# A Fourier mixing layer and a gated feed-forward layer on one core: when the filters and the last third of the weights are loaded, and how many filler matmuls run

## The chip, the cores and the metric

The kernel runs on one core of one Trainium2 chip. The metric is the device time in microseconds (us) of one execution. The time before is 983.68 us, the median of 4 runs (981.99 to 984.23).

The engines are named as in the profile: PE is the matrix engine (TensorE), DVE the vector engine, ACT the scalar engine, POOL the GpSimd engine, and SP the engine that issues most of the DMA transfers.

## The reference, cut to what matters

```python
# x: (8, 3008, 256); filt_r, filt_i: (1505, 256)
X = np.fft.rfft(x, axis=1)
Y = X * (filt_r + 1j * filt_i)[None]
y = np.fft.irfft(Y, n=3008, axis=1).reshape(24064, 256)
out = np.maximum(y @ w_gate, 0.0) * (y @ w_val) @ w_out    # w_gate, w_val: (256, 1536), w_out: (1536, 256)
```

## The kernel before

The transform of length 3008 is done as 94 x 32, in matmuls. For each of the 8 batches, stage A multiplies x by a table of cosines and sines (`psA`) and stores the result to DRAM (`Abuf`). It is loaded again in another order, in four slabs (`at`). This round trip is called the bounce of A. Stage B makes the second transform (`psX`), multiplies by the filters (`tt`, `uu`) and transforms back (`psD`). A second bounce through DRAM (`Dbuf`, `dC`) leads to stage C (`psY`). Then come the matmuls of the feed-forward layer (`psV`, `psG`, `psO`).

From batch 1 on, all this is woven into the feed-forward matmuls of the batch before. Batch 0 has nothing to hide behind. The change concerns only this start, which I call the prologue.

The parts that matter:

```python
    def load_filters(half):            # 8 DMAs per half (half 0 has 4 small ones more), fp32 -> bf16, issued by POOL
        ...
                nc.gpsimd.dma_start(dst[r:r + 31:2, gs, :], ...)
                nc.gpsimd.dma_start(dst[r + 1:r + 32:2, gs, :], ...)
        ...
    def place_filters(half):           # the other rows are a copy of these
        ...
                if half == 0:
                    nc.vector.tensor_copy(dst[r + 32:r + 64, gs, :], dst[r:r + 32, gs, :])
                else:
                    nc.sync.dma_start(dst[r + 32:r + 64, gs, :], dst[r:r + 32, gs, :])
        ...
    def load_vg(c):                    # one third of w_val and of w_gate, issued by POOL
        ...
    def hold_gpsimd(tile_):            # a tiny copy: POOL, and all that it issues later, waits for this tile
        scr = pro.tile([32, 8], tile_.dtype, tag="scr", bufs=1)
        nc.gpsimd.tensor_copy(scr, tile_)
        ...
    def items_b(b, junk=0):            # stage B, 12 items
        ...
            nc.vector.tensor_tensor(tt, psX, Ftr[:, g:g + 2, :], op=ALU.mult)
            if b == 0 and g % 4 == 2:  # every second item: uu on POOL, by way of ACT
                xs = pro.tile([128, 2, D], FP32, tag="xs", bufs=2)
                nc.scalar.copy(xs, psX)
                nc.gpsimd.tensor_tensor(uu, xs, Fti[:, g:g + 2, :], op=ALU.mult)
            else:
                nc.vector.tensor_tensor(uu, psX, Fti[:, g:g + 2, :], op=ALU.mult)
        ...
    def warm(n):                       # n matmuls on constants, to keep PE's clock up
        ...
    load_x(0, nc.sync, 2 * q)
    ...
    hold_gpsimd(XF[0][0:32, 0:8])      # the first slice of x
    load_filters(0)
    load_filters(1)
    ...
    hold_gpsimd(ats[0][64:96, NG - 1, 0:8])      # the third slab of the bounce of A
    load_vg(0)
    load_vg(1)
    for f in items_b(0, 2):
        f()
    warm(26)
    load_d(0)
    hold_gpsimd(dCs[0, 0][0:32, 0, 0:8])         # the first slice of the bounce of D
    load_vg(2)
    load_o()
    load_x(1, nc.gpsimd)
```

## Time and profile before

| what | before |
|---|---|
| time, median of 4 runs | 983.68 us |
| span of the profiled run | 980.1 us |
| stage A, PE back to back | 7.9 to 24.9 us |
| bounce of A, PE idle for 8.55 us of it | 25.5 to 37.9 us |
| stage B | 38.0 to 54.4 us |
| bounce of D | 55.3 to 59.8 us |
| wait for the last third of the weights ends | 68.2 us |
| from 80 us on | PE without gaps |

First the page of the kernel before: the busy times of the engines, the clock that was granted to PE in 40 slices of the span (9 is 90% or more), and the shares of the chain of work that ended last.

```profile
PE 962.2 (98%) x6817; PEld 664.2 (68%) x6820; DVE 577.2 (59%) x1046; ACT 556.6 (57%) x1191; POOL 51.8 (5%) x86
...
PEclk9899999999999999999999999999999999999999
...
PE 96%; DMA 2%; issue 1%; DVE 0%; ACT 0%; POOL 0%; SPq 0%; POOLq 0%; ACTq 0%
```

PE is busy for 98% of the span, and the chain is PE for 96%. Only the first slices can give anything.

Next the chain of waits of the kernel before in the first 90 us, in order of time: start, duration, and what the chain passed through.

```profile
25.52 6.19 DMA Abuf_71<-asb
...
33.55 4.28 DMA Fti<-Fti
...
37.96 0.58 PE psX L274 x2
...
54.07 5.72 issue
...
60.69 7.45 DMA WgT<-in_moe_w_gate_dram
...
68.18 0.49 PE psG L345 x2
```

The chain leaves PE at three places. Two DMAs follow each other in the bounce of A. (The one called `Fti<-Fti` is named by its place in the queue; the matmul `psX` after it needs the last slab `at`, which landed at the same time.) "issue" at 54.07 is the bounce of D, during which PE runs filler. And the load of `WgT` ends at 68.14 us.

Now PE's timeline of the same run: start, duration, engine, line, operation; in brackets the idle time before and what ended it.

```profile
16.34 1.02 PE L243 MATMUL psA<-XF_89,WA 128*96 128x512 f32 x2
...
37.96 0.58 PE L274 MATMUL psX<-at,F_91 128*128 128x256 bf16 x2 [8.55 <-DMA Fti<-Fti]
...
47.00 0.27 PE L293 MATMUL psD<-tt,I2t 128*128 128x256 bf16 x1
47.24 0.27 PE L294 MATMUL psD<-uu,I2u 128*128 128x256 bf16 x1
...
68.18 0.49 PE L345 MATMUL psG<-yT,WgT 128*128 128x376 bf16 x2 [0.78 <-DMA WgT<-in_moe_w_gate_dram]
```

The second half of x (`XF_89`) is used at 16.34 us with no wait. It is loaded by three DMAs, issued at 5.91, 7.43 and 8.47 us. The view of this tile gives, of the time from issue to landing, the least, the median and the most:

```profile
L154 SPq DMA_DIRECT2D XF_89<-in_x_dram x3: 469/469/527, 5.9 to 8.5; - x3
...
DMA to landing us min/median/max: 6.0/6.8/7.7
```

Within stage B, the matmul at 47.24 starts 0.05 us after a `uu` of POOL has ended (46.03 + 1.16 = 47.19). The last line is the wait for the last third of the weights.

POOL's timeline shows when it issues what:

```profile
7.57 0.18 POOL L227 COPY scr<-XF_88 32x8 f32<-32x8 f32 x1 [3.24 <-DMA XF_88<-in_x_dram]
8.16 0.71 POOL L186 DMA_DIRECT2D Ftr<-in_filt_r_dram  x1 [0.41 <-issue]
...
18.38 0.52 POOL L192 DMA_DIRECT2D Ftr<-in_filt_r_dram  x1 [5.69 <-DVE I2t L176]
...
28.50 0.69 POOL L188 DMA_DIRECT2D Fti<-in_filt_i_dram  x1
...
46.03 1.16 POOL L281 TENSOR_TENSOR uu<-xs,Fti 128x512 bf16<-128x512 f32 x1 [1.14 <-ACT xs L280]
48.32 1.16 POOL L281 TENSOR_TENSOR uu<-xs,Fti 128x512 bf16<-128x512 f32 x1 [1.14 <-ACT xs L280]
...
59.81 0.18 POOL L227 COPY scr<-dC 32x8 bf16<-32x8 bf16 x1 [5.74 <-DMA dC<-Dbuf_79]
...
60.69 0.71 POOL L215 DMA_DIRECT2D WgT<-in_moe_w_gate_dram  x1
```

In stage B POOL makes one `uu` every 2.30 us. At 59.81 us the hold on the bounce of D is released, and only then the last third of the weights is issued.

### The profile page before, as it was taken

How to read it: one execution, taken by the hardware profiler on the slowest of the kernel's cores; microseconds unless marked ns; L12 is line 12 of the kernel's file. 1: busy time of each engine (PE TensorE's matmuls, PEld its weight loads, DVE VectorE, ACT ScalarE, POOL GpSimd, SP SyncE). 2: the span in 40 equal slices, each digit the busy share in tenths (PEclk: the TensorE clock that was granted, in tenths of full speed). 3: DMA queues.
4: the chain of work that ended last, by engine and by line, in shares of the span. 5: the costliest groups of instructions: out<-in, count | busy, mean ns of one | idle time of the engine just before them, and what ended most of it. 6: DMA issues, size and time to landing. Idle time of an engine off the chain costs nothing.

```text
span 980.1 us, 18332 instructions
## 1 busy us (share of the span) xinstructions
PE 962.2 (98%) x6817; PEld 664.2 (68%) x6820; DVE 577.2 (59%) x1046; ACT 556.6 (57%) x1191; POOL 51.8 (5%) x86
## 2 busy tenths in 40 slices
PE   8689999999999999999999999999999999999998
PEld 3355677667775677757776577765777567777776
DVE  4543486448753496536855378543875448655554
ACT  3245665556655556555655556555665555655554
POOL 5430000010000000000000100001000000000000
PEclk9899999999999999999999999999999999999999
DMA  9984924182413814156231653317332241411111
GB/s 261 202 210 145 246 59 121 49 238 67 123 50 96 211 54 129 32 144 162 76 113 32 169 132 86 103 44 223 85 103 70 60 118 54 129 33 33 33 33 48
DMA packets 96825, 107.20 MB, mean 109 GB/s; under 512 B 6212, under 2 KB 85508, under 8 KB 95108
## 3 DMA queue, kind: packets, MB, share of 16 engines
q1 hardware_dynamic: 87760, 78.97, 29.0%
q0 software_dynamic: 8576, 25.86, 10.4%
q8 instruction: 53, 0.87, 0.4%
q10 hardware_dynamic: 400, 1.20, 0.3%
q14 instruction: 36, 0.29, 0.1%
HBM read 59.31 MB, written 49.81 MB: 111 GB/s over the span
## 4 chain that ended last, share of the span: by engine, by line
PE 96%; DMA 2%; issue 1%; DVE 0%; ACT 0%; POOL 0%; SPq 0%; POOLq 0%; ACTq 0%
PE psO L365 26%; PE psV L345 25%; PE psG L345 25%; PE psA L243 11%; PE psX L274 2%; PE psY L328 2%; PE psD L294 2%; PE psD L293 2%; PE psJ L382 1%; DMA WgT<-in_moe_w_gate_dram 1%; DMA Abuf_71<-asb 1%; DMA Fti<-Fti 0%; SPq L208 0%; POOL uu L281 0%; DVE XF_88 L386 0%
## 5 line engine op out<-in xcount | busy, mean ns | idle before, releaser
L350 DVE SCALAR_TENSOR_TENSOR prod<-psG,vsb 128x376 bf16<-128x376 f32 x768 | 421.4, 550 | 358.8 <-ACT vsb L348 348.3
L348 ACT CAST vsb<-psV 128x376 bf16<-128x376 f32 x768 | 363.5, 473 | 211.3 <-PE psV L345 210.0
L365 PE MATMUL psO<-WoT,prod 128*128 128x256 bf16 (+1 forms) x2304 | 375.1, 273 | 0.0
L345 PE MATMUL psV<-yT,WvT 128*128 128x376 bf16 x1536 | 370.4, 322 | 1.0 <-ACT yT L334 0.4
L345 PE MATMUL psG<-yT,WgT 128*128 128x376 bf16 x1536 | 369.8, 322 | 0.8 <-DMA WgT<-in_moe_w_gate_dram 0.8
L365 PEld LDWEIGHTS <-prod 128*128 128x128 bf16 (+1 forms) x2304 | 246.1, 110 | 89.9
L345 PEld LDWEIGHTS <-WgT 128*128 128x128 bf16 x1536 | 149.6, 97 | 96.6 <-DMA WgT<-in_moe_w_gate_dram 1.2
L345 PEld LDWEIGHTS <-WvT 128*128 128x128 bf16 x1536 | 143.2, 98 | 67.4 <-issue 54.9
L246 ACT CAST asb<-psA 96x512 bf16<-96x512 f32 x128 | 74.3, 582 | 100.7 <-PE psA L243 98.5
L296 ACT CAST dsb<-psD 128x512 bf16<-128x512 f32 x96 | 56.2, 586 | 50.4 <-PE psD L294 48.6
L370 ACT COPY osb<-psO 128x512 f32<-128x512 f32 (+1 forms) x128 | 61.6, 481 | 19.9 <-PE psO L365 13.5
L277 DVE TENSOR_TENSOR tt<-psX,Ftr 128x512 bf16<-128x512 f32 x96 | 65.4, 682 | 10.0 <-PE psX L274 10.0
L243 PE MATMUL psA<-XF_88,WA 128*96 128x512 f32 x128 | 65.4, 592 | 0.0
L243 PE MATMUL psA<-XF_89,WA 128*96 128x512 f32 x128 | 65.4, 592 | 0.0
L283 DVE TENSOR_TENSOR uu<-psX,Fti 128x512 bf16<-128x512 f32 x90 | 61.3, 681 | 0.0
L294 PE MATMUL psD<-uu,I2u 128*128 128x256 bf16 x192 | 47.1, 272 | 1.3 <-POOL uu L281 1.3
L293 PE MATMUL psD<-tt,I2t 128*128 128x256 bf16 x192 | 47.3, 272 | 0.1
L328 PEld LDWEIGHTS <-dC 96*128 96x128 bf16 x512 | 35.8, 97 | 14.8 <-issue 12.0
L274 PE MATMUL psX<-at,F_91 128*128 128x256 bf16 x192 | 37.3, 277 | 8.6 <-DMA Fti<-Fti 8.6
L328 PE MATMUL psY<-M_90,dC 96*128 96x94 bf16 x512 | 42.3, 204 | 0.0
L336 DVE CAST yT<-psY 128x376 bf16<-128x376 f32 x64 | 34.6, 541 | 12.1 <-PE psY L328 12.1
L334 ACT CAST yT<-psY 128x376 bf16<-128x376 f32 x64 | 30.2, 472 | 19.6 <-PE psY L328 19.6
(48 smaller groups left out, 205.1 us busy)
## 6 DMA issues: line engine op xcount, KB each, us to landing
out_dram<-osb SPq DMA_DIRECT2D x64, 256.0 KB, 2.2
XF_88<-in_x_dram POOLq DMA_DIRECT2D x20, 512.0 KB, 7.0
XF_89<-in_x_dram POOLq DMA_DIRECT2D x20, 512.0 KB, 6.7
out_dram<-osb SPq DMA_DIRECT2D x64, 120.0 KB, 1.9
XF_88<-in_x_dram SPq DMA_DIRECT2D x6, 256.0 KB, 4.3
XF_89<-in_x_dram SPq DMA_DIRECT2D x3, 512.0 KB, 6.8
Abuf_71<-asb SPq DMA_DIRECT2D x4, 384.0 KB, 6.1
at<-Abuf_71 SPq DMA_DIRECT2D x4, 384.0 KB, 6.4
```

The lines of the kernel that those rows point to most:

```text
L243: nc.tensor.matmul(psA[0:NROW], WA[:, :NROW], XF[c * NC2 // NX2][:, o:o + 512], start=True, stop=True)
L246: nc.scalar.copy(dst, psA[0:NROW])
L277: nc.vector.tensor_tensor(tt, psX, Ftr[:, g:g + 2, :], op=ALU.mult)
L283: nc.vector.tensor_tensor(uu, psX, Fti[:, g:g + 2, :], op=ALU.mult)
L293: nc.tensor.matmul(psD[:, i], I2t[:, g + i, :], tt[:, i], start=True, stop=False)
L294: nc.tensor.matmul(psD[:, i], I2u[:, g + i, :], uu[:, i], start=False, stop=True)
L328: nc.tensor.matmul(psY[:, j * N1:(j + 1) * N1], dCs[b, z][:, j, h * 128:(h + 1) * 128], M1, start=True, stop=True)
L345: nc.tensor.matmul(pt[:, :W], w[:, h, ft * 128:(ft + 1) * 128], yt[:, h, :], start=(h == 0), stop=(h == 1))
L348: nc.scalar.copy(vsb, psV[:, :W])
L350: nc.vector.scalar_tensor_tensor(prod, in0=psG[:, :W], scalar=0.0, in1=vsb, op0=ALU.max, op1=ALU.mult)
L365: nc.tensor.matmul(psO[:tw, t % 2], prods[ft][:, t * 128:t * 128 + tw], WoT[:, ft, :], start=(ft == 0), stop=(ft == NFT - 1))
L370: nc.scalar.copy(osb[:tw, :n], psO[:tw, :n])
```

## The change

The intent is to use the time before x has landed for the filters, to keep weights off the DMA engines while the last slab travels, to have the last third of the weights there before it is needed, and to spend fewer matmuls on keeping the clock up (four fewer in all).

```diff
--- before.py
+++ after.py
@@ -396,7 +396,6 @@
     for (src, dst) in FILT:
         for g in (H - 1, NG - 1):
             nc.vector.memset(dst[64:128, g, :], 0.0)
-    hold_gpsimd(XF[0][0:32, 0:8])
     load_filters(0)
     load_filters(1)
 
@@ -409,21 +408,22 @@
         if i % 4 == 3 and i > 3:
             load_at(0, i // 4 - 1)
     load_at(0, 3)
-    warm(20)
+    warm(26)
     place_tables(0)
     place_filters(0)
     place_tables(1)
     place_filters(1)
-    hold_gpsimd(ats[0][64:96, NG - 1, 0:8])
+    hold_gpsimd(ats[0][96:128, NG - 1, 0:8])
     load_vg(0)
     load_vg(1)
 
-    for f in items_b(0, 2):
+    for i, f in enumerate(items_b(0, 1)):
         f()
-    warm(26)
+        if i == 4:
+            load_vg(2)
+    warm(28)
     load_d(0)
     hold_gpsimd(dCs[0, 0][0:32, 0, 0:8])
-    load_vg(2)
     load_o()
     load_x(1, nc.gpsimd)
     for h in range(2):
```

## The prediction

> **What bounds it.** From 80 us on the kernel is TensorE-bound: the busy line gives PE 962.2 of 980.1 us, and the chain of waits PE 96%. The change touches only the first 72 us. There (chain of waits, timeline):
> - Stage A, 7.9 to 24.9 us: PE back to back. The last slice of x lands about 14.5 and is needed at 16.3.
> - Bounce, 25.5 to 37.9: last store of A 6.19 us, last slab load 6.2 us. PE idles 8.55 us; its clock is 0.5 from 34.3 to 41.1.
> - Stage B, 38.0 to 54.4: 2.30 us per two items, a latency loop DVE tt, ACT xs, POOL uu (1.16 us), PE psD, psX: PE waits 0.13 us for each POOL uu. Junk is not in it.
> - Bounce of D: loads land 59.8; 26 junk matmuls end at 60.05, 0.25 us later.
> - First block: PE stalls 1.3 us to 68.2 for the last third of the weights.
>
> **What the change does.**
> 1. Filters: without the hold (released 7.57) the first issue moves from 8.2 to 4.4 us, its packets from 11.4 to about 7.6. DMA is not idle there: share 0.83 to 0.97 under x, 1.2 to 1.3 later. The Trainium skill, "DMA: Bandwidth & Descriptors", "Queues, rings and completion order", says that engines round-robin between queues by packet; the trace agrees: beside x and the tables filters got 35 to 90 512-byte packets per us, nearly alone 350. So about 270 packets, 0.8 us of full-rate work, move forward; x slips up to 1 us inside its 1.8 us of slack. Filters end 1 to 1.5 us sooner, the last slab about 1.0 sooner (estimate; -0.5 to 2.5).
> 2. First weights held for the last slab: their packets began only at 38.0, so 0. POOL issues 1.9 us later, having had 1.9 us idle before its first uu: 0.
> 3. Last third of the weights inside stage B: 1.43 us of issue in a POOL gap of 1.14; 0.3 to 0.5 us on one uu, mostly absorbed. The first block's stall goes: gain 1.2.
> 4. One junk matmul per item instead of two: at the slow clock PE once held DVE up 0.59 us: gain 0.5. Period stays 2.30.
> 5. 28 junk matmuls instead of 26 before C, 0.213 us each: cost 0.4. Six more before stage B fall in idle time; PE still idles 6 us, so the clock still drops ("TensorE: Matmul & The Clock Gate", "What's actually happening": half clock after an idle window of about 3.4 us; here it fell 4.9 us after the last matmul). That costs little, as PE isn't stage B's bound.
>
> Sum: 1.0 + 1.2 + 0.5 - 0.4 = about 2.4 us, all critical.
>
> **Prediction: 981.2 us, 978.4 to 983.7 in 8 of 10. Faster by over 2%: 0.01; within 2%: 0.98; slower: 0.01.**
>
> **What would show it.** Filter issues from 4.4 us; stage A ends at 24.9 (0 to 0.5 later); first psX near 37; uu period 2.30; last psD 16 us after first psX; no weight wait in the first block; junk ends 0.6 us after D's first load; the rest 2.4 us earlier.
>
> **What would make it wrong.** x slipping past its slack and stalling stage A; filters finishing far sooner (first psX near 35, and with PE idle under 4 us no clock drop: 3 to 4 us won); weight issues delaying the uu loop; the weights' traffic slowing the stores of D.

## More of the kernel before

The filters' first DMA is issued at 8.16 us, after the hold was released; the ninth waits until 18.38, and the last goes out at 28.50.

Last, what the DMA queues moved from 4 to 15 us: packets, MB, and the time of their packets as a share of the 16 engines. q1 is the queue of SP (x and the bounce), q0 that of POOL (here the filters), q10 that of ACT (tables).

```profile
q1 hardware_dynamic: 411, 3.00, 77.2%
q10 hardware_dynamic: 81, 0.37, 9.1%
q0 software_dynamic: 200, 0.10, 6.6%
```

x has these 11 us nearly to itself; the filters have moved 200 packets of 512 bytes.

## The result, and the profile after

| | before | changed kernel |
|---|---|---|
| median (range) | 983.68 us (981.99 to 984.23, 4 runs) | 980.49 us (980.18 to 981.28, 4 runs) |
| ratio of the means | | 0.9972 (0.9954 to 0.9989) |

A ratio here is the mean time of one kernel's fast runs over that of the other's of the same rounds, so it is not quite the ratio of the medians. The change is a gain of some 2.8 us (0.28%). The total was close to the forecast of 2.4 us. The way there was not.

The chain of waits of the changed kernel in the first 90 us:

```profile
4.00 5.64 DMA XF_88<-in_x_dram
...
9.65 8.50 DMA XF_89<-in_x_dram
...
18.29 1.07 PE psA L243 x2
...
27.52 5.42 DMA Abuf_71<-asb
...
34.79 3.86 DMA Fti<-Fti
...
38.81 0.59 PE psX L274 x2
...
55.38 5.78 PE psJ L382 x26
61.16 0.18 PE psY L328 x4
```

The chain now begins with x. Its second half occupies the chain from 9.65 to 18.15 us. Stage A therefore ends 2 us later: the last store to `Abuf` begins at 27.52 instead of 25.52 us. That store and the slab load behind it are shorter than before. Yet the first `psX` comes at 38.81 us, 0.85 us later than before, not 1 us sooner as predicted. Near 61 us the chain runs through the 28 filler matmuls, which end after the data has come. The load of `WgT` is gone.

PE's timeline of the changed kernel:

```profile
18.29 1.07 PE L243 MATMUL psA<-XF_89,WA 128*96 128x512 f32 x2 [1.37 <-DMA XF_89<-in_x_dram]
...
38.81 0.59 PE L274 MATMUL psX<-at,F_91 128*128 128x256 bf16 x2 [6.10 <-DMA Fti<-Fti]
...
48.06 0.27 PE L294 MATMUL psD<-uu,I2u 128*128 128x256 bf16 x1 [0.71 <-POOL uu L281]
```

PE waits for `XF_89`. (The 1.37 us in brackets are what the profile counts as idle before the line; the start itself moved from 16.34 to 18.29 us.) The last line shows PE waiting 0.71 us for a `uu`. PE has less filler, so it reaches the wait sooner.

POOL's timeline of the changed kernel:

```profile
4.27 0.71 POOL L186 DMA_DIRECT2D Ftr<-in_filt_r_dram  x1
...
11.77 0.52 POOL L192 DMA_DIRECT2D Ftr<-in_filt_r_dram  x1 [2.97 <-DMA Ftr<-in_filt_r_dram]
...
19.36 0.51 POOL L192 DMA_DIRECT2D Fti<-in_filt_i_dram  x1 [5.97 <-DMA Ftr<-in_filt_r_dram]
...
28.54 0.60 POOL L188 DMA_DIRECT2D Fti<-in_filt_i_dram  x1
...
45.34 0.77 POOL L215 DMA_DIRECT2D WvT<-in_moe_w_val_dram  x1
46.09 0.72 POOL L215 DMA_DIRECT2D WgT<-in_moe_w_gate_dram  x1
46.83 1.18 POOL L281 TENSOR_TENSOR uu<-xs,Fti 128x512 bf16<-128x512 f32 x1
```

The first filter DMA is issued 3.9 us earlier than before. But the compiled program gives POOL's DMAs eight completion counters in turn, so the ninth issue waits for the first to land, the tenth for the second, and so on. The eleventh waits until 19.36 us, and the last goes out at 28.54 us against 28.50 before. The head start of the issues is lost by then. The last third of the weights is issued at 45.34 and 46.09 us, inside stage B, and the `uu` behind it starts directly afterwards.

The DMA queues of the changed kernel from 4 to 15 us:

```profile
q1 hardware_dynamic: 373, 2.65, 75.0%
q0 software_dynamic: 670, 0.32, 22.2%
q10 hardware_dynamic: 43, 0.20, 4.5%
```

The filters have moved 670 packets by 15 us instead of 200, but SP's queue has moved 2.65 MB instead of 3.00. The filters' share of the engines' time went from 6.6% to 22.2%.

### The profile page after: what moved, and what is told of

It is laid out like the page before. It is cut to its first block, busy times and chain, and to the rows that moved or that the text cites. A ratio compares the mean times of both kernels' runs of the same rounds, so it can differ in the third digit from the quotient of the medians.

```text
span 979.5 us, 18320 instructions
## 1 busy us (share of the span) xinstructions
PE 961.9 (98%) x6814; PEld 664.0 (68%) x6816; DVE 576.9 (59%) x1046; ACT 556.7 (57%) x1191; POOL 51.4 (5%) x85
## 4 chain that ended last, share of the span: by engine, by line
PE 95%; DMA 2%; POOL 1%; DVE 0%; ACT 0%; issue 0%; SPq 0%; DVEq 0%; ACTq 0%; POOLq 0%
PE psO L365 26%; PE psV L345 25%; PE psG L345 25%; PE psA L243 11%; PE psY L328 2%; PE psX L274 2%; PE psD L294 2%; PE psD L293 2%; PE psJ L382 1%; DMA XF_89<-in_x_dram 1%; DMA XF_88<-in_x_dram 1%; DMA Abuf_71<-asb 1%; DMA Fti<-Fti 0%; POOL uu L281 0%; DVE tt L277 0%
## 5 line engine op out<-in xcount | busy, mean ns | idle before, releaser
L328 PEld LDWEIGHTS <-dC 96*128 96x128 bf16 x512 | 35.8, 97 | 14.7 <-issue 12.3
L274 PE MATMUL psX<-at,F_91 128*128 128x256 bf16 x192 | 37.6, 278 | 6.1 <-DMA Fti<-Fti 6.1
```

The source lines that it names most:

```text
L328: nc.tensor.matmul(psY[:, j * N1:(j + 1) * N1], dCs[b, z][:, j, h * 128:(h + 1) * 128], M1, start=True, stop=True)
```

## The experiments

The theories at the outset were these. Theory 1 is the prediction: the filters' earlier start wins about 1 us in the bounce. Theory 2 came from the first trace after: the filters hold x up, stage A gives away what the bounce wins, and the gain comes from the weights. Where single parts cost 1 us or less, intervals of runs are as wide as the effect; so the traces' milestones are used beside them. The table has one trace of each run. All times are in us; "stage A ends" is the end of ACT's last copy, after which the last store begins, "first psX" is where the bounce of A ends, "to C" the time from the last `psD` to the first `psY`, and "first block" the time from its first to the next block's first `psV`.

```
kernel                 stage A  bounce  first   stage  to C   first   first psA of   span
                       ends     of A    psX     B             block   batch 1 to end
before                  25.5    12.5    38.0    16.4   5.72    9.64   900.1          980.1
c0_before_again         25.9    11.8    37.7    16.9   5.72   10.06   900.0          980.5
e5_last_slab_only       25.4    12.4    37.9    16.4   5.72   11.02   900.0          981.1
e2_third_in_b_only      25.4    11.6    36.9    16.8   5.72    8.33   900.1          978.0
e4_junk_only            26.3    11.4    37.7    16.0   6.15   10.49   900.3          980.9
e3_after_hold_kept      25.9    11.6    37.5    16.1   6.15    8.33   900.1          978.4
e1_filters_only         26.8    10.8    37.6    16.7   5.78    9.86   900.0          980.1
changed kernel          27.5    11.3    38.8    16.0   6.15    8.34   900.0          979.5
e0_after_again          27.2    10.6    37.8    15.7   6.15    8.33   900.4          978.6
e0c_after_third         27.1    10.7    37.7    16.1   6.15    8.33   900.0          978.5
e8_hold_for_last_x      25.1    13.8    38.9    18.1   5.72   10.75   900.1          983.7
e6_split_and_24         25.2    12.3    37.5    15.8   5.68    8.34   900.2          977.7
e7_copies_on_vector     26.2    10.8    37.0    16.3   5.38    8.33   899.7          977.0
e9_xs_first             25.6    11.8    37.4    14.2   5.80    8.34   899.7          975.7
```

The column before the last says that from batch 1 on nothing changes: 899.7 to 900.4 us in all fourteen traces. The first `psA` itself starts between 7.3 and 8.5 us, with no relation to the edits, and shifts the columns "stage A ends" and "first psX" by as much.

There were three calls of four kernels. The kernel before was run with each, and its median was 983.58, 981.93 and 982.70 us (11 runs each). Medians of different calls should therefore not be compared directly. All kernels gave correct results.

### The changed kernel again (e0_after_again, e0c_after_third)

No edit.

> The changed kernel once more, unedited, for the size of the gain and for a second trace of it. Theory 1 (filters win time in the bounce): gain over before 2 to 3.5 us, and this trace shows stage A ending near 25.5 us and the first psX near 37, the first trace (27.5 and 38.8) having been an unlucky run. Theory 2 (filters hold x up and win nothing): stage A again ends 1.5 to 2 us later than before's 25.5 and the first psX lies at 38 or later; the gain over before is then 1 to 2 us, all of it from the first block.

> The changed kernel, unedited, a third time, beside e9 and e8 on the same chip. Ratio to before 0.997 to 0.998, stage A ending at 26.8 to 27.5 us and first psX at 37.6 to 38.8 as in the two traces so far; if the stall of stage A was chance, it ends at 25.5.

Measured: 981.04 us, ratio 0.9978 (0.9964 to 0.9993), and 980.32 us, ratio 0.9971 (0.9955 to 0.9987). Stage A ended at 27.2 and 27.1 us. The stall of stage A is not chance: it stands in all three traces. The gain is that of the first result. Both theories had a point: the gain was as large as theory 1 had it, with the stage A of theory 2.

### The filters alone (e1_filters_only)

```diff
-    hold_gpsimd(XF[0][0:32, 0:8])
     load_filters(0)
```

> Before without the hold on the filters, nothing else. Theory 1: 0.5 to 1.5 us faster than before, first psX at 36.5 to 37.3. Theory 2: no gain or a loss of up to 1 us (stage A stalls about 2 us for x, and the store and slab load after it are 1 to 2 us shorter); first psX at 38 to 39.

Measured: 982.11 us against 983.58, ratio 0.9994 (0.9977 to 1.001): no gain that can be told from nothing. In PE's timeline of e1, the first line is the first `psX`, the second the wait for the last third of the weights, which is still there:

```profile
37.63 0.59 PE L274 MATMUL psX<-at,F 128*128 128x256 bf16 x2 [6.87 <-DMA at<-Abuf]
...
68.43 0.49 PE L345 MATMUL psG<-yT,WgT 128*128 128x376 bf16 x2 [0.73 <-DMA WgT<-in_moe_w_gate_dram]
```

The first `psX` came at 37.63 us, between the two theories.

### The changed kernel with the hold kept (e3_after_hold_kept)

```diff
+    hold_gpsimd(XF[0][0:32, 0:8])
     load_filters(0)
```

> The changed kernel with the hold on the filters put back. Theory 1: 0.5 to 1.5 us slower than the changed kernel. Theory 2: as fast as the changed kernel or up to 1 us faster, with stage A ending at 25.5 and the first psX at 38.

Measured: 980.19 us, ratio 0.9967 (0.9954 to 0.9981). In the same call the changed kernel took 981.04 us. The means of six runs each are 980.09 and 981.03, a difference of 0.94 with a standard error of 0.34 us. So putting the hold back makes the changed kernel faster, not slower. From the chain of waits of e3, the last store of A and the first `psX`:

```profile
25.89 5.82 DMA Abuf<-asb
...
37.47 0.58 PE psX L274 x2
```

Theory 1 falls for this step. Over the traces, with the hold and an otherwise equal bounce (before, c0, e2, e3, e4, e5, e6) stage A ends at 25.7 us and the first `psX` comes at 37.6 us on average. Without the hold (e1 and the changed kernel three times) these are 27.2 and 38.0 us. The bounce itself is 1.1 us shorter, as the prediction had it, and stage A ends 1.5 us later (counted from its first `psA` it lasts 17.9 against 19.3 us). The 0.4 us between the two first `psX` is within the scatter of the traces (36.9 to 38.0 and 37.6 to 38.8 us): shown is that nothing is won there.

### The hold moved the other way (e8_hold_for_last_x)

```diff
-    hold_gpsimd(XF[0][0:32, 0:8])
+    hold_gpsimd(XF[1][64:96, 0:8])
```

> Before with the filters held for the last slice of x instead of the first: the other direction. If DMA work in the first 38 us is merely reordered, x lands by about 14.5 us, stage A ends at 25 to 25.8, the bounce grows by up to 1 us for the later filters, and the time is within 0.7 us of before. If an early start of the filters is worth anything, it is 1 us or more slower, the last filter landing 2 to 3 us later.

Measured: 985.06 us against 982.70, ratio 1.0016 (0.9997 to 1.0035). In PE's timeline of e8, the first `psX` and the wait for weights:

```profile
38.91 0.58 PE L274 MATMUL psX<-at,F 128*128 128x256 bf16 x2 [9.90 <-DMA at<-Abuf]
...
71.92 0.49 PE L345 MATMUL psG<-yT,WgT 128*128 128x376 bf16 x2 [0.74 <-DMA WgT<-in_moe_w_gate_dram]
```

The ratio leaves open whether it is slower at all, but the trace has the first `psX` at 38.91 us, 1.3 us later than the average with the old hold, and a stage B of 18.1 us. At 48.92 us DVE waits 0.83 us for a copy of the filters (`Fti<-Fti`). So in this one trace the later start cost time, while the earlier start was paid for by x; that the old hold is the best place is not shown.

### The last third of the weights alone (e2_third_in_b_only)

```diff
-    for f in items_b(0, 2):
+    for i, f in enumerate(items_b(0, 2)):
         f()
+        if i == 4:
+            load_vg(2)
     ...
     hold_gpsimd(dCs[0, 0][0:32, 0, 0:8])
-    load_vg(2)
```

> Before with the last third of the weights issued after the fifth item of stage B, nothing else. Both theories: the wait for weights in the first block (about 1.3 us) goes; gain 0.8 to 1.3 us. If POOL's issues in stage B cost the loop more than thought, stage B grows from 16.4 to 17 us or more and the gain is under 0.6.

Measured: 980.46 us against 983.58, ratio 0.9974 (0.996 to 0.9988), a gain of about 2.6 us. This one part gains about as much as the whole change did. The first block took 8.33 us, as in all traces without the wait. With the wait it took 9.64 us in the trace that the prediction was made from, but 9.86, 10.06, 10.49, 10.75 and 11.02 us in the five other traces that have it. The wait costs 1.3 to 2.7 us, 2.0 on average; the prediction's 1.2 us came from the trace with the smallest. The first `psX` of e2 was also the earliest of all (36.92 us), by nothing that this edit does, so its interval rather than its median should be believed.

### The filler matmuls alone (e4_junk_only)

```diff
-    warm(20)
+    warm(26)
     ...
-    for f in items_b(0, 2):
+    for f in items_b(0, 1):
         f()
-    warm(26)
+    warm(28)
```

> Before with only the junk matmuls changed (20 to 26, 2 to 1 per item, 26 to 28). The prediction costs these at +0.5 and -0.4 us: within 0.5 us of before, 0.9995 to 1.0005. Rival: if the shorter idle of PE or the lighter stage B matters more, 1 us or more faster (0.999 or less). In the trace: uu period 2.30 us as before, stage B about 0.5 us shorter, first psY about 6.1 us after the last psD instead of 5.7.

Measured: 981.58 us against 981.93, ratio 0.999 (0.9977 to 1.0003): inconclusive by the runs, and the interval holds both expectations. The traces are clearer. With two filler matmuls per item stage B took 16.6 us on average (before, c0, e1, e2, e5), with one 16.0 us (e3, e4 and the changed kernel three times), near the 0.5 us predicted. It lies where the prediction had it, at the beginning, where PE's clock is at half: POOL's first two `uu` start 2.61 us apart on average with two filler matmuls and 2.07 with one, the later ones 2.30 us apart in both groups. The way from the last `psD` to the first `psY` grew from 5.72 to 6.15 us, the 0.4 us predicted. In e4 PE's timeline shows what became of the rest:

```profile
66.93 0.49 PE L345 MATMUL psV<-yT,WvT 128*128 128x376 bf16 x2 [0.44 <-DMA WvT<-in_moe_w_val_dram]
68.87 0.49 PE L345 MATMUL psG<-yT,WgT 128*128 128x376 bf16 x2 [1.45 <-DMA WgT<-in_moe_w_gate_dram]
```

PE arrives earlier at weights that have not landed, and waits 0.44 and 1.45 us.

### The first two thirds held for the last slab, alone (e5_last_slab_only)

```diff
-    hold_gpsimd(ats[0][64:96, NG - 1, 0:8])
+    hold_gpsimd(ats[0][96:128, NG - 1, 0:8])
```

> Before with the first two thirds of the weights held for the last slab instead of the third, nothing else. Prediction: 0 (0.9995 to 1.0005), as their packets came after the last slab anyway. Rival: it frees the last slab load of traffic, 0.5 us or more faster; or the later issues hold up the first uu, 0.5 us or more slower.

Measured: 982.53 us against 982.70, ratio 0.9993 (0.9978 to 1.0008). The first `psX` at 37.9 us and stage B of 16.4 us are those of before. Its first block is the longest of the six with the wait for weights (11.02 us); whether by the edit or by chance one trace cannot say. By the runs nothing was won or lost, as predicted.

### The kernel before again (c0_before_again)

No edit; a control.

> The kernel before, unedited: a control of the method, and a second trace of it. Ratio 1.000 within its interval. Runs of before have spread over 3.5 us (981.5 to 985.0), those of the kernels without the wait for the last third of the weights over 1 to 2 us. Theory A (the wait for that third is itself what varies): a trace of a slow run shows that wait grown to 2 us or more and stages A and B as in the first trace. Theory B (the bounce of A varies): a slow run has its first psX late instead, at 39 us or more.

Measured: 982.52 us against 981.93, ratio 1.0002 (0.9989 to 1.0016). The traced run took 982.31 us, so it was not a slow one, and theories A and B about the slow runs were not decided by it. Its first block was 10.06 us, 0.4 us longer than in the first trace, which speaks for A, but that is one trace. The granted clock of the runs, told at the end of the next section, bears on this too.

### Further from there (e6_split_and_24, e7_copies_on_vector, e9_xs_first)

e6 keeps the hold, issues the last third of the weights in two halves and ends the filler before C in time:

```diff
-        if i == 4:
-            load_vg(2)
-    warm(28)
+        if i in (4, 6):
+            load_vg(2, (i // 2 - 2,))      # one of w_val, w_gate
+    warm(24)
```

> The changed kernel with the hold on the filters kept, the last third of the weights issued in two halves (one after the fifth item of stage B, one after the seventh, 0.7 us each, so that each fits the 1.14 us gap of POOL), and 24 junk matmuls before C instead of 28. Expected 0.7 to 1.3 us faster than the changed kernel with the hold kept (980.2): 979.0 to 979.5, with PE's waits for uu back to 0.2 us or less in the middle of stage B, and the first psY 5.4 us after the last psD instead of 6.1. If the two halves' delays are absorbed anyway, only the 0.6 us of junk is won.

Measured: 979.45 us, ratio 0.9972 (0.9961 to 0.9984). The median lies where it was expected, but on a chip where the kernel before was faster too; by the ratio nothing is won over e3 (0.9967). The expectation on PE's waits missed: PE still waits 0.62 to 0.95 us for a `uu`, as it does in e4 (0.77 to 0.88), where no weights are issued in stage B. Those waits come from PE having less filler and not from POOL's issues. The way to C was 5.68 instead of 6.15 us (5.4 was expected).

e7 also makes the four copies of the second half of the filters on DVE instead of by DMA:

```diff
-                if half == 0:
-                    nc.vector.tensor_copy(dst[r + 32:r + 64, gs, :], dst[r:r + 32, gs, :])
-                else:
-                    nc.sync.dma_start(dst[r + 32:r + 64, gs, :], dst[r:r + 32, gs, :])
+                nc.vector.tensor_copy(dst[r + 32:r + 64, gs, :], dst[r:r + 32, gs, :])
```

> e6 with the four copies of the second half of the filters (192 KB each, by DMA within SBUF, in flight beside the last slab load) made on the vector engine instead. Theory: the last slab load is held up by other traffic, so taking these away brings it home 0.5 to 1.5 us sooner, and the kernel gains as much over e6. Rival: the slab load waits for the filters' own traffic, or the vector engine's first multiply now waits for the last filter to land (about 36 us) plus its copy (0.95 us): no gain, or a loss up to 1 us.

Measured: 978.89 us, ratio 0.9969 (0.9956 to 0.9981). In this trace x came late (first `psA` at 8.48 us), the bounce took 10.8 us instead of 12.3 in e6, and the first `psX` came 0.4 us earlier. The gain over e6 is 0.46 us with a standard error of 0.40: not shown.

e9 is e7 with ACT's copy `xs` put ahead of DVE's `tt`, because both read `psX` and the trace of before has the copy waiting for `tt` in all six items. The Trainium skill, "PSUM — Partial Sum Buffer", section "PSUM bank collisions raise a hardware error", says that the compiler's scheduler makes accesses of two engines to one bank of PSUM, in the same 32 partitions, depend on one another, reads included; the trace agrees, and the order is then the program's to choose:

```diff
-            nc.vector.tensor_tensor(tt, psX, Ftr[:, g:g + 2, :], op=ALU.mult)
             if b == 0 and g % 4 == 2:
                 xs = pro.tile([128, 2, D], FP32, tag="xs", bufs=2)
                 nc.scalar.copy(xs, psX)
+            nc.vector.tensor_tensor(tt, psX, Ftr[:, g:g + 2, :], op=ALU.mult)
+            if b == 0 and g % 4 == 2:
                 nc.gpsimd.tensor_tensor(uu, xs, Fti[:, g:g + 2, :], op=ALU.mult)
```

> e7 with the scalar engine's copy xs put ahead of the vector engine's tt for the items whose uu POOL makes. Theory (stage B is a latency loop tt, xs, uu, psD, psX): 0.7 us of tt leaves the loop, the period of uu falls from 2.3 to 2.1 us per two items, stage B from 16.3 to 14.5 to 15.3 us and the kernel gains 1 to 1.8 us over e7. Rival (stage B is bound by PE or DVE work): period 2.3 as before, gain under 0.5.

Measured: 978.14 us against 982.70, ratio 0.9948 (0.9933 to 0.9963). In the same call the changed kernel took 980.32 us; the means differ by 2.20 us with a standard error of 0.29. This version beats both kernels. The 2.20 us are those of all its edits together. e7 was run in another call; against it stand the ratios (0.9948 and 0.9969, with intervals that overlap) and one trace each, whose spans are 975.7 and 977.0 us. POOL's timeline of e9, three `uu` in a row:

```profile
46.43 1.17 POOL L280 TENSOR_TENSOR uu<-xs,Fti 128x512 bf16<-128x512 f32 x1
48.30 1.16 POOL L280 TENSOR_TENSOR uu<-xs,Fti 128x512 bf16<-128x512 f32 x1 [0.69 <-ACT xs L277]
50.20 1.15 POOL L280 TENSOR_TENSOR uu<-xs,Fti 128x512 bf16<-128x512 f32 x1 [0.75 <-ACT xs L277]
```

They are 1.9 us apart, where before they were 2.30 us apart (46.03 and 48.32), a shorter period than the 2.1 us expected, and stage B fell from 16.3 us in e7 (15.8 in e6) to 14.2. That stage B was a latency loop through `tt`, `xs`, `uu` and `psD` is thereby shown: no work was taken away, only one operation out of the loop. What limits it now was not tested. From 45.1 to 50.9 us of e9 DVE's operations follow each other with pauses of less than 0.1 us, so DVE has little left to give there.

## Why the prediction was right or wrong

The predicted time, 981.2 us with a range of 978.4 to 983.7, holds the measured 980.49, and the forecast of 2.4 us is near the measured 2.8 (3.2 by the medians). Point by point:

1. **Filters.** The step that failed is "x slips up to 1 us inside its 1.8 us of slack", and with it "the last slab about 1.0 sooner". The mechanism was named rightly. The Trainium skill, "DMA: Bandwidth & Descriptors", section "Queues, rings and completion order", has each DMA engine go round between the queues by packet; this trace fits, with the filters' share of the engines at 22.2% instead of 6.6% beside x, though it does not show the single turns. Its size was wrong on both sides. The slack was not 1.8 us: the prediction has the last slice of x land "about 14.5" (close to the 14.27 us of the second of the three loads), but the third landed at 16.14, 0.2 us before it was needed at 16.34. Over the seven traces with the hold it landed at 14.2 to 16.5 us, and in e3 PE had to wait for it even so, by some 0.6 us. And the slip was more than 1 us: 470 packets moved ahead, not 270, and in the four traces without the hold the last slice landed at 18.15, 17.88, 17.72 and 17.50 us, each time 0.13 to 0.14 us before PE went on with it. The bounce did shrink by about 1.1 us, as the prediction's 1.0. Stage A ended 1.5 us later, and in the sum the first `psX` came no sooner (38.0 against 37.6 us, within the scatter). The single runs and e3 agree: nothing gained alone (0.9994), 0.94 us lost within the changed kernel. The filters' own head start did not last either: the first issue was 3.9 us earlier, the last one level in this trace (28.54 and 28.50 us), since every issue from the ninth on waits for one eight places before it. In the three other traces without the hold the last issue was at 27.3 (twice) and 28.2 us. The last filter landed at 36.6 us in the changed kernel and at 33.7 (twice) and 35.5 us in these three, against 34.8 to 35.7 us with the hold. Why exactly the bounce got shorter was not taken apart; that it starts later beside the same filter traffic fits.
2. **First weights held for the last slab.** Predicted 0, measured 0 (0.9993, and neither the first `psX` nor stage B moved).
3. **Last third of the weights.** Right in mechanism, mis-sized: predicted 1.2, measured 2.0 us in the traces (1.3 to 2.7) and 2.6 us in e2's runs (1.2 to 3.9 by its interval). The wait was read from one trace, and that trace had the smallest of six. The predicted loss on one `uu` was absorbed: the `uu` behind the weights' issues (POOL's third, that of the sixth item) in the changed kernel starts 8.0 us after the first `psX` (46.83 less 38.81), as before (46.03 less 37.96).
4. **One filler matmul per item.** Predicted 0.5, traces 0.6. The period indeed stayed at 2.30 us after the first two `uu`.
5. **28 instead of 26 before C.** Predicted a cost of 0.4, measured 0.43 in every trace that has them. The clock still dropped, as predicted from the page "TensorE: Matmul & The Clock Gate", section "What's actually happening" (half clock after an idle window of about 3.4 us): in the three traces of the changed kernel it fell to half at 36.2 to 37.7 us. In the first of them that was 3.8 us after the last filler matmul, before the change 4.9.

So two errors cancelled, and that the total came out near the forecast was luck: 1.0 us was expected from the filters and did not come, and the weights gave about as much more. The signs named in the prediction told it: the first `psX` "near 37" and stage A "0 to 0.5 later" both failed, and "no weight wait", "junk ends 0.6 us after D's first load" and "last psD 16 us after first psX" held.

What stays open: the traces add up to less than the runs. The mean span of the two traces of before is 980.3 us, that of the three of the changed kernel 978.9, a gain of 1.4 us, while the means of the runs differ by 2.3 to 2.8. Both traced runs of before (981.87 and 982.31 us) lie below its median of 982.70 over all 37 runs, which reach 986.56. Where the slowest runs of before lose their time was not seen, because none of them was traced. But the record lists each run's granted clock, and time goes with it (correlation -0.90 over the 39 runs of before, c0 included, that have one): the 24 runs at 0.996 or more take 982.1 us on average, the 15 below it 984.3. All 16 runs of the changed kernel have 0.996 or more, and take 980.7 us. At like clock the gain is thus 1.4 us, that of the traces; the rest of the 2.3 to 2.8 us is runs of before with a lower clock. The one traced run with a low clock (e8, 0.994, 985.49 us) has 10.2 us at half clock about the end of the bounce, where 12 of the other 13 traces have 6.8. Whether the lower clock costs this time itself or only marks a longer wait is not shown, nor why the changed kernel was spared it.

## What to carry to other kernels

A load that is started earlier beside another one need not be free: if the other load has a deadline, find when its last part lands (not the median part), how late it may come, and how much of the DMA engines' time the newcomer takes, packet by packet, before calling the time "unused". A wait read from one trace is a sample; take a second trace before costing it, and judge parts by undoing them one at a time, since a total near the forecast can hide two errors. Where engines pass data round a loop, take an operation out of the loop (here by the order of two instructions) before removing work beside it.

## What the Trainium skill lacked or had wrong

- "DMA: Bandwidth & Descriptors", "Queues, rings and completion order": it says that engines change between queues by packet, and that a packet holds several descriptors, but has no measured figure for what a queue of small transfers takes from one of large ones. Here 670 packets with 0.32 MB took 22.2% of the engines' time in 11 us, and the large queue moved 2.65 instead of 3.00 MB.
- The same page, "Latency and other measured facts", gives about 1 us to the first byte for POOL's DMAs, without saying from when it counts. Here the first packet of POOL's queue came 2.1 us after the first issue began in the changed kernel (6.38 less 4.27) and 3.4 us after it before (11.58 less 8.16), beside x; of this the issue itself is 0.7 us. In e8, where the issue came after x had landed, it was 1.9 us (18.41 less 16.47). The page does not say that its figure depends on other traffic; the cause of the difference was not tested. The figures are from the packet records of the traces.
- "TensorE: Matmul & The Clock Gate", "What's actually happening": nothing to correct, the traces agree with its window. Half clock began 3.3 to 5.3 us after the last filler matmul (whose end is modelled). The first stretch at half clock lasted 6.8 us in twelve of the fourteen traces, 3.4 us in one and 10.2 us in one, all multiples of 3.4.
